# Leftover token blocks of two ranges multiplied as a pair, and a last product moved to the end

## The chip, the cores and the metric

The kernel runs on one core of a Trainium2 chip. Its engines run side by side: TensorE (PE) multiplies matrices, VectorE (DVE) and ScalarE (ACT) read and write tiles, GpSimd (POOL) copies and casts here and issues transfers, SyncE (SP) issues transfers. The metric is the time of one execution on the device in microseconds (us); a kernel's time is the median of several runs.

## The reference

Attention over 8 batches, 12 heads, 448 tokens and head width 64, and behind it a two-layer network on all 3584 tokens (768 to 2048 to 768) with a leaky rectifier:

```python
attn = softmax(q @ k.T / sqrt(64))          # per batch and head
x = (attn @ v) as [3584, 768]               # heads side by side
h = x @ w_in                                # [3584, 2048]
g = np.maximum(0.01 * h, h)
out = g @ w_out                             # [3584, 768]
```

Inputs and output are 32-bit floats; the kernel multiplies in bf16 and adds in 32 bits.

## The kernel before

**Units and clusters.** Attention is cut into 48 units, one pair of heads of one batch each. A unit has four chunks of scores. A *cluster* is a bundle of attention work, put in between the network's matmuls: score matmuls of three chunks (six matmuls of 448 columns into three of the `sc` tiles), their exponentials on ACT (the third one is emitted late, by `settle`), and the products with v of earlier chunks (`pv`, 16 matmuls for each head), which DVE normalises into `x`. Before its scores a unit's q and k are loaded (units below 18 in pairs by POOL's queue, later ones singly by SP's), cast or copied on POOL (`cast`), and transposed: up to unit 13 by PE, from unit 14 by a DMA that SP issues (`turn`). The finished `x` of a unit is transposed into `xT`, from unit 9 on by such a DMA too. SP issues in order; so do its waits.

**Ranges.** The network runs over 8 ranges of tokens, cut at multiples of 128 (`cuts`). Even ranges have 384 tokens (3 blocks of 128), odd ones 512 (4 blocks). For each range, `mlp(i)` first computes h: 16 groups of 6 matmuls (L326) into one of two `g` banks of PSUM, each followed by the rectifier on ACT (L470, in range 0 L458). h is one tile of 4 blocks, allocated anew for each range.

**Second layer.** A block times `w_out` is done in two halves of 384 columns. `blocks` (L438) does it plainly: 16 matmuls of 384 columns for each half, 32 for a block, with a copy by DVE (L442) behind each half. `block_pair` (L367) does two blocks together by Winograd's form of Strassen's scheme: 7 half products of 8 matmuls in place of 8, 56 matmuls in place of 64. For it DVE forms sums and differences of the blocks of h (`mix_h`, L348 to L351, four instructions for four groups of h) and, once, in range 1, of the quarters of the weights (`mix_weights`, L339, 16 instructions into `w_mix`). Seven evictions on DVE (copies L373, additions L376) bring a pair to its two output tiles `o1` and `o2`; there are three `o` buffers, and SP stores them.

Range 0 does its three blocks by `blocks`. The other even ranges (2, 4, 6) do one block by `blocks` and two as a pair; odd ranges are two pairs: 11 pairs and 6 single blocks.

**Order.** The order of PE's work is written out by the program: `mlp` yields after each piece how much it did, and the loop at the end puts the next cluster in when the share of the range's work done reaches the cluster's share. In range 0 it goes by the number of pieces done instead (`early`). A pair can take a cluster after its fourth product (without its value products, which are made up for later) and after its last.

**The end.** In the last pair, the last product goes in two pieces of 192 columns, each with its own copy and its own store, split over ACT's and SP's queues:

```python
            piece(slice(0, NW // 2))
            put(slice(0, NW // 2))
            done = product(a, s4, w_out_sb[:, hi, right])
            join(o1, right, a)
            store(o1, cuts[i] + one.start)
            piece(slice(NW // 2, NW))
            put(slice(NW // 2, NW))
```

Of the kernel before, what the change touches and what calls it, by code (L numbers as in the profile page):

```python
# [10 lines left out]
BF16 = mybir.dt.bfloat16  # L11
AX = mybir.ActivationFunctionType
# [4 lines left out]
def kernel(  # L17
# [9 lines left out]
    nc = tc.nc  # L27

    B, H, S, D = q.shape
    DM, DF = moe_w_in.shape  # L30
    P = 128
# [3 lines left out]
    KD = DM // P  # L35
    MD = DF // P
    NW = DM // 2
# [3 lines left out]
    cuts = [((b * S) // P) * P for b in range(B)] + [B * S]  # L41
# [13 lines left out]
    h_pool = ctx.enter_context(tc.tile_pool(name="h", bufs=1))  # L55
# [30 lines left out]
    w_in_sb = w_pool.tile([P, KD, DF], BF16)  # L86
    w_out_sb = w_pool.tile([P, MD, DM], BF16)
    MH = MD // 2
    w_mix = w_pool.tile([P, 4, MH, NW], BF16)
    h_mix = h_pool.tile([P, 3, MH, 2 * P], BF16, name="hmix")  # L90
    w_in_v = moe_w_in.rearrange("(ko ki) n -> ki ko n", ki=P)
    w_out_v = moe_w_out.rearrange("(ko ki) n -> ki ko n", ki=P)

# [217 lines left out]
    def settle():  # L311
        while late:
            expo(*late.pop(0))
# [17 lines left out]
    def mix_weights():  # L331

        for m in range(0, MH, 2):
            lo, hi = slice(m, m + 2), slice(MH + m, MH + m + 2)
            w11, w12 = w_out_sb[:, lo, :NW], w_out_sb[:, lo, NW:]
            w21, w22 = w_out_sb[:, hi, :NW], w_out_sb[:, hi, NW:]
            t1, t2, t3, t4 = (w_mix[:, x, lo] for x in range(4))
            for o, x, y in ((t1, w12, w11), (t2, w22, t1), (t3, w22, w12), (t4, w21, t2)):
                nc.vector.tensor_sub(o, x, y)  # L339
                yield  # L340

    def mix_h(h, m, nh):

        lo, hi = slice(m, m + 2), slice(MH + m, MH + m + 2)
        h11, h21 = h[:, lo, :nh], h[:, lo, nh:2 * nh]
        h12, h22 = h[:, hi, :nh], h[:, hi, nh:2 * nh]
        s2, s3, s4 = (h_mix[:, x, lo, :nh] for x in range(3))
        nc.vector.tensor_sub(s3, h11, h21)  # L348
        nc.vector.tensor_add(h21, h21, h22)
        nc.vector.tensor_sub(s2, h21, h11)  # L350
        nc.vector.tensor_sub(s4, h12, s2)  # L351

    def block_pair(i, h, c, nh):

        lo, hi = slice(0, MH), slice(MH, MD)
        one, two = ts(c, P), slice(nh + c * P, nh + (c + 1) * P)
        s2, s3, s4 = (h_mix[:, x, :, one] for x in range(3))
        t1, t2, t3, t4 = (w_mix[:, x] for x in range(4))
        left, right = slice(0, NW), slice(NW, DM)
        o1 = o_pool.tile([P, DM], F32, name="o")  # L360
        o2 = o_pool.tile([P, DM], F32, name="o")
        b, a = next_bank(), next_bank()

        def product(ps, x, w, first=False):
            settle()
            for m in range(MH):
                nc.tensor.matmul(  # L367
                    ps[:, :NW], x[:, m], w[:, m], start=(first and m == 0), stop=(m == MH - 1), skip_group_check=True,
                )
            return MH * NW  # L370

        def keep(o, at, ps):
            nc.vector.tensor_copy(o[:, at], ps[:, :NW])  # L373

        def join(o, at, ps):
            nc.vector.tensor_add(o[:, at], o[:, at], ps[:, :NW])  # L376
# [16 lines left out]
        t0 = cuts[i] + two.start  # L393
        if t0 + P == B * S:
            store(o2, t0, right)

            def piece(w):
                settle()
                for m in range(MH):
                    nc.tensor.matmul(  # L400
                        b[:, w], h[:, MH + m, two], t4[:, m, w], start=False, stop=(m == MH - 1),
                        skip_group_check=True,
                    )

            def put(w):
                nc.vector.tensor_copy(o2[:, w], b[:, w])
                store(o2, t0, w, (nc.scalar, nc.sync))

            piece(slice(0, NW // 2))
            put(slice(0, NW // 2))  # L410
            done = product(a, s4, w_out_sb[:, hi, right])
            join(o1, right, a)
            store(o1, cuts[i] + one.start)
            piece(slice(NW // 2, NW))
            put(slice(NW // 2, NW))
            return
        done = product(a, s4, w_out_sb[:, hi, right])
        join(o1, right, a)
        store(o1, cuts[i] + one.start)
# [7 lines left out]
    def blocks(i, h, todo):  # L427

        o = {}
        n = cuts[i + 1] - cuts[i]  # L430
        for c, w in todo:
            settle()
            if c not in o:
                o[c] = o_pool.tile([P, DM], F32, name="o")
            ps = next_bank()
            nw = w.stop - w.start
            for m in range(MD):
                nc.tensor.matmul(  # L438
                    ps[:, :nw], h[:, m, ts(c, P)], w_out_sb[:, m, w],
                    start=(m == 0), stop=(m == MD - 1),  # L440
                )
            nc.vector.tensor_copy(o[c][:, w], ps[:, :nw])  # L442
            t0 = cuts[i] + c * P
            if w.stop == DM:
                store(o.pop(c), t0)
            yield MD * nw, True

    def mlp(i):

        n = cuts[i + 1] - cuts[i]  # L450
        h = h_pool.tile([P, MD, 4 * P], BF16, name="h")
        if i == 0:
            for m in opened:
                part(i, m, (KD - 1,))
            for m in range(MD):
                if m not in opened:
                    part(i, m, range(KD))
                nc.scalar.activation(h[:, m, :n], open_t.pop(m)[:, :n], AX.Prelu, alpha=0.01)  # L458
                settle()
                yield KD * n, True  # L460
            yield from blocks(i, h, [(c, slice(w, w + NW)) for w in (0, NW) for c in range(n // P)])
            return

        nh = n // (2 * P) * P
        weights = mix_weights() if i == 1 else iter(())
        ready = []
        for m in range(MD):
            mm = m // 2 + m % 2 * MH
            part(i, mm, range(KD))
            nc.scalar.activation(h[:, mm, :n], open_t.pop(mm)[:, :n], AX.Prelu, alpha=0.01)  # L470
            settle()
            if ready:
                mix_h(h, ready.pop(), nh)
# [4 lines left out]
        mix_h(h, ready.pop(), nh)  # L478
        for c in range(2 * nh // P, n // P):
            yield from blocks(i, h, [(c, slice(0, NW)), (c, slice(NW, DM))])  # L480
        for c in range(nh // P):
            yield from block_pair(i, h, c, nh)


    def supply(u):
# [106 lines left out]

    begin = [9, 8 * 2 + 3] + [8 * (i + 1) + 5 for i in range(2, B - 1)] + [8 * B + 3]

    early = [4, 6, 8, 10, 12, 14, 16, 18, 20, 22]
    for i in range(B):
        work = list(range(begin[i], begin[i + 1])) if i + 1 < B else []
        n = cuts[i + 1] - cuts[i]
        pairs = n // (2 * P) if i > 0 else 0
        total = MD * KD * n + (n // P - pairs / 4) * MD * DM  # L600
        if i == B - 2:
            total *= 0.75
        used, done, groups = 0, 0, 0
# [50 lines left out]
```

## Time and profile before

| | us |
|---|---|
| median of 3 runs | 408.59 (408.35 to 408.76) |
| the profiled execution | 408.24 |
| its span | 406.5 |
| range 0, from its first group to its end | 31 to 79.8 |
| range 1 | 79.8 to 135.1 |
| range 2 | 135.1 to 178.3 |
| range 3 | 178.3 to 230.0 |
| range 4 | 230.0 to 273.3 |
| range 5 | 273.3 to 325.0 |
| range 6 | 325.0 to 361.7 |
| range 7 | 361.7 to the end |

The span is the time from the first to the last instruction in the profile; the execution's time has some 1.7 us around it. A group of instructions in the profile has a line, an engine, an operation, the tiles it writes and reads, its shape and count, then its busy time, the mean of one in ns, and the idle time in front of it with what ended that. On the chain of waits a row is a start, a length and what ran.

### The profile page before, as it was taken

The numbers are of one execution on the slowest core, as the hardware profiler recorded it, in microseconds if no ns is written. First come the engines' busy times: TensorE is split into PE (matmuls) and PEld (weight loads), VectorE is DVE, ScalarE is ACT, GpSimd is POOL, SyncE is SP. The second block draws the span as 40 slices with busy tenths as digits, with TensorE's granted clock in tenths as the row PEclk, the third lists the DMA queues.
The fourth block names the chain that finished last, engine by engine and source line by source line (L and its number), as shares of the span: only waits on it lengthen the run. The fifth ranks groups of instructions, "written<-read, shape, count | busy, mean of one in ns | idle before, by whom it ended". The sixth has DMA issues, their size and how long they took to land.

```text
span 406.5 us, 9142 instructions
## 1 busy us (share of the span) xinstructions
PE 393.6 (97%) x3655; PEld 228.4 (56%) x3672; DVE 173.0 (43%) x457; ACT 228.3 (56%) x324; POOL 110.0 (27%) x177
## 2 busy tenths in 40 slices
PE   7999999999999999999999999999999999999994
PEld 3566666555555665554555665655455566654562
DVE  3662432465743344334344344443344434323442
ACT  5998872487554776456742677447644476014300
POOL 8786754523312231113112133213110000000000
PEclk9999999999999999999999999999999999999998
DMA  8999999994838784898647678587563411120022
GB/s 129 194 201 205 202 200 127 192 275 110 175 109 207 195 196 97 218 198 139 166 102 170 162 188 159 138 212 178 123 105 101 104 44 24 50 81 0 2 77 77
DMA packets 96586, 57.23 MB, mean 141 GB/s; under 512 B 53280, under 2 KB 93088, under 8 KB 96544
## 3 DMA queue, kind: packets, MB, share of 16 engines
q1 hardware_dynamic: 76848, 44.15, 47.1%
q0 software_dynamic: 19392, 12.26, 21.2%
q8 instruction: 28, 0.46, 0.5%
q10 hardware_dynamic: 304, 0.25, 0.2%
q14 instruction: 14, 0.11, 0.1%
HBM read 45.61 MB, written 11.01 MB: 139 GB/s over the span
## 4 chain that ended last, share of the span: by engine, by line
PE 92%; DVE 3%; ACT 1%; DMA 1%; issue 1%; DVEq 0%; ACTq 0%; POOLq 0%
PE g L326 35%; PE g L367 25%; PE g L271 12%; PE sc L252 10%; PE g L438 8%; PE g L235 1%; ACT e L261 1%; DVE x L279 1%; DMA fq<-in_q_dram 1%; PE g L292 1%; DVE rec L278 1%; PE sc L326 0%; PE g L400 0%; DVE xT L293 0%; DVE qkb L146 0%
## 5 line engine op out<-in xcount | busy, mean ns | idle before, releaser
L261 ACT ACTIVATE e<-sc 112x896 bf16<-112x896 f32 x192 | 165.3, 918 | 88.4 <-PE sc L252 88.1
L326 PE MATMUL g<-xT,w_in_sb 128*128 128x384 bf16 (+1 forms) x739 | 148.8, 352 | 2.2 <-DVE x L279 1.1
L326 PEld LDWEIGHTS <-w_in_sb 128*128 128x128 bf16 x768 | 72.9, 98 | 65.7 <-issue 2.1
L470 ACT ACTIVATE h<-g 128x512 bf16<-128x512 f32 (+1 forms) x112 | 61.9, 552 | 60.0 <-PE g L326 57.6
L271 PEld LDWEIGHTS <-e 112*128 112x128 bf16 x1536 | 56.2, 98 | 22.1 <-issue 15.6
L271 PE MATMUL g<-v,e 112*128 112x65 bf16 x1536 | 64.0, 194 | 0.3 <-ACT e L261 0.2
L252 PE MATMUL sc<-qkT 64*128 64x448 bf16 x384 | 50.0, 353 | 1.1 <-DVE qkT L241 0.6
L146 POOL CAST qkb<-fq 112x512 bf16<-112x512 f32 x30 | 18.6, 621 | 111.0 <-DMA fq<-in_q_dram 82.9
L278 DVE RECIPROCAL rec<-g 112x4 f32<-112x4 f32 x96 | 17.4, 181 | 68.1 <-PE g L271 46.4
L367 PEld LDWEIGHTS <-h 128*128 128x128 bf16 x344 | 33.4, 98 | 22.7 <-issue 0.6
L279 DVE TENSOR_TENSOR x<-g,rec 112x256 bf16<-112x256 f32 x96 | 40.7, 424 | 3.6 <-DVE rec L278 0.3
L373 DVE COPY o<-g 128x384 f32<-128x384 f32 x43 | 24.0, 557 | 29.7 <-PE g L367 29.0
L367 PEld LDWEIGHTS <-hmix 128*128 128x128 bf16 x264 | 25.1, 98 | 19.3 <-issue 3.6
L148 POOL CAST v<-fv 112x512 bf16<-112x512 f32 x30 | 19.1, 636 | 60.8 <-PE g L271 50.6
L438 PE MATMUL g<-w_out_sb,h 128*128 128x384 bf16 x192 | 32.7, 326 | 0.4 <-DVE x L279 0.3
L367 PE MATMUL g<-w_mix,hmix 128*128 128x384 bf16 x176 | 32.3, 326 | 0.0
L367 PE MATMUL g<-w_out_sb,h 128*128 128x384 bf16 x176 | 30.4, 326 | 0.4 <-DVE x L279 0.4
L367 PE MATMUL g<-w_mix,h 128*128 128x384 bf16 x168 | 30.7, 326 | 0.0
L376 DVE TENSOR_TENSOR o<-o,g 128x384 f32<-128x384 f32 x33 | 18.3, 554 | 28.6 <-PE g L367 28.6
L252 PEld LDWEIGHTS <-qkT 64*128 64x128 bf16 x384 | 14.5, 94 | 20.1 <-issue 11.0
L438 PEld LDWEIGHTS <-h 128*128 128x128 bf16 x192 | 18.5, 98 | 12.3 <-issue 0.6
L348 DVE TENSOR_TENSOR hmix<-h 128x512 bf16<-128x512 bf16 (+1 forms) x28 | 11.8, 420 | 31.5 <-ACT h L470 31.5
(50 smaller groups left out, 199.3 us busy)
## 6 DMA issues: line engine op xcount, KB each, us to landing
fk<-in_k_dram SPq DMA_DIRECT2D x31, 224.0 KB, 3.3
fq<-in_q_dram SPq DMA_DIRECT2D x30, 224.0 KB, 3.3
fv<-in_v_dram SPq DMA_DIRECT2D x30, 224.0 KB, 3.8
w_in_sb<-in_moe_w_in_dram POOLq DMA_DIRECT2D x4, 768.0 KB, 11.1
w_out_sb<-in_moe_w_out_dram POOLq DMA_DIRECT2D x4, 768.0 KB, 13.5
out_dram<-o SPq DMA_DIRECT2D x7, 336.0 KB, 3.5
out_dram<-o SPq DMA_DIRECT2D x8, 288.0 KB, 3.9
out_dram<-o SPq DMA_DIRECT2D x8, 240.0 KB, 3.3
```

The source lines that it names most:

```text
L146: by(qk_sb[u][:, x].rearrange("p so h d -> p h so d"), f)
L148: by(v_sb[u % NV][:, :, :, :D], f)
L252: nc.tensor.matmul(ps[:, j, :S], t[j * D:(j + 1) * D, S + c * SC:S + c * SC + P], t[j * D:(j + 1) * D, :S], start=True, stop=True,)
L261: nc.scalar.activation(e[:, :, c, :], sc_t.pop((u, c))[:SC, :, :S], AX.Exp, scale=scale)
L271: nc.tensor.matmul(ps[:, qc, :], e[:, at:at + P], vt[:, j, c, :], start=(c == 0), stop=(c == NSC - 1),)
L278: nc.vector.reciprocal(rec, ps[:SC, :, D:])
L279: nc.vector.tensor_mul(x_t[u][:, :, j, :], ps[:SC, :, :D], rec.to_broadcast([SC, NSC, D]))
L326: nc.tensor.matmul(open_t[m][:, :n], w_in_sb[:, kk, ts(m, P)], xT[:, kk, at:at + n], start=(fresh and kk == kks[0]), stop=(kk == KD - 1),)
L367: nc.tensor.matmul(ps[:, :NW], x[:, m], w[:, m], start=(first and m == 0), stop=(m == MH - 1), skip_group_check=True,)
L373: nc.vector.tensor_copy(o[:, at], ps[:, :NW])
L438: nc.tensor.matmul(ps[:, :nw], h[:, m, ts(c, P)], w_out_sb[:, m, w], start=(m == 0), stop=(m == MD - 1),)
L470: nc.scalar.activation(h[:, mm, :n], open_t.pop(mm)[:, :n], AX.Prelu, alpha=0.01)
```

## The change

The tile h is kept for the whole kernel and has five blocks in place of four, `h[:, :, 0:640]`. Range 0 writes its blocks to slots 2, 3 and 4 and multiplies only the first two. Range 2 writes to slots 0 to 2 and does two pairs: slots (0, 1), and (4, 2), the kept third block of range 0 with its own third. Range 4 writes to slots 2 to 4, does one pair (2, 3), and keeps its third block for range 6, which does as range 2. So there are 13 pairs and 2 single blocks. `spots(i)` gives a range's first slot and its pairs, `token(i, x)` the first token of a slot.

The tile of one weight mixture (t1 = w12 - w11) is no longer separate: DVE writes it over w12 in the right half of `w_out`, after range 0 has used it, and the order of the four mixtures is changed to suit.

The loop's total for a range is counted from its pairs, and the last three entries of `early` are 17, 18, 19 in place of 18, 20, 22.

In the last pair the s4 product comes ahead of both pieces of the last product, and the store of `o1` goes out in two halves.

```diff
-    w_mix = w_pool.tile([P, 4, MH, NW], BF16)
-    h_mix = h_pool.tile([P, 3, MH, 2 * P], BF16, name="hmix")
+    w_mix = w_pool.tile([P, 3, MH, NW], BF16)
+    KEEP = 4
+    h = h_pool.tile([P, MD, (KEEP + 1) * P], BF16, name="h")
+    h_mix = h_pool.tile([P, 3, MH, 2, P], BF16, name="hmix")
...
-            t1, t2, t3, t4 = (w_mix[:, x, lo] for x in range(4))
-            for o, x, y in ((t1, w12, w11), (t2, w22, t1), (t3, w22, w12), (t4, w21, t2)):
+            t2, t3, t4 = (w_mix[:, x, lo] for x in range(3))
+            for o, x, y in ((t3, w22, w12), (w12, w12, w11), (t2, w22, w12), (t4, w21, t2)):
...
-    def mix_h(h, m, nh):
-
+    def spots(i):
+
+        n = cuts[i + 1] - cuts[i]
+        if n == 4 * P:
+            return 0, [(0, 2), (1, 3)]
+        if i == 0:
+            return 2, []
+        return (0, [(0, 1), (KEEP, 2)]) if i % 4 == 2 else (2, [(2, 3)])
+
+    def token(i, x):
+
+        if x == KEEP:
+            return cuts[i - i % 4] + 2 * P
+        return cuts[i] + (x - spots(i)[0]) * P
+
+    def mix_h(i, m):
+
+        at = spots(i)[1]
+        step = [max(1, at[-1][y] - at[0][y]) for y in range(2)]
+        one, two = (slice(at[0][y], at[-1][y] + 1, step[y]) for y in range(2))
         lo, hi = slice(m, m + 2), slice(MH + m, MH + m + 2)
-        h11, h21 = h[:, lo, :nh], h[:, lo, nh:2 * nh]
-        h12, h22 = h[:, hi, :nh], h[:, hi, nh:2 * nh]
-        s2, s3, s4 = (h_mix[:, x, lo, :nh] for x in range(3))
+        t = h.rearrange("p m (c t) -> p m c t", t=P)
+        h11, h21 = t[:, lo, one], t[:, lo, two]
+        h12, h22 = t[:, hi, one], t[:, hi, two]
+        s2, s3, s4 = (h_mix[:, x, lo, :len(at)] for x in range(3))
...
         if t0 + P == B * S:
+            store(o1, token(i, x1), left)
             store(o2, t0, right)
...
-            piece(slice(0, NW // 2))
-            put(slice(0, NW // 2))
-            done = product(a, s4, w_out_sb[:, hi, right])
-            join(o1, right, a)
-            store(o1, cuts[i] + one.start)
-            piece(slice(NW // 2, NW))
-            put(slice(NW // 2, NW))
+            done = product(a, s4, w_out_sb[:, hi, right])
+            join(o1, right, a)
+            store(o1, token(i, x1), right)
+            for w in (slice(0, NW // 2), slice(NW // 2, NW)):
+                for m in range(MH):
+                    nc.tensor.matmul(
+                        b[:, w], h[:, MH + m, two], t4[:, m, w], start=False, stop=(m == MH - 1),
+                        skip_group_check=True,
+                    )
+                nc.vector.tensor_copy(o2[:, w], b[:, w])
+                store(o2, t0, w, (nc.scalar, nc.sync))
...
-            yield from blocks(i, h, [(c, slice(w, w + NW)) for w in (0, NW) for c in range(n // P)])
+            yield from blocks(i, [(first + c, slice(w, w + NW)) for w in (0, NW) for c in range(2)])
...
-        for c in range(2 * nh // P, n // P):
-            yield from blocks(i, h, [(c, slice(0, NW)), (c, slice(NW, DM))])
-        for c in range(nh // P):
-            yield from block_pair(i, h, c, nh)
+        for c in range(len(pairs)):
+            yield from block_pair(i, c)
...
-    early = [4, 6, 8, 10, 12, 14, 16, 18, 20, 22]
+    early = [4, 6, 8, 10, 12, 14, 16, 17, 18, 19]
...
-        pairs = n // (2 * P) if i > 0 else 0
-        total = MD * KD * n + (n // P - pairs / 4) * MD * DM
+        total = MD * KD * n + (len(spots(i)[1]) * 7 / 4 if i > 0 else 2) * MD * DM
```

More of the change, by code (lines that the diff above doesn't have):

```diff
@@ L351, in mix_h, with block_pair @@
         nc.vector.tensor_sub(s4, h12, s2)
-    def block_pair(i, h, c, nh):
+    def block_pair(i, c):
         lo, hi = slice(0, MH), slice(MH, MD)
-        one, two = ts(c, P), slice(nh + c * P, nh + (c + 1) * P)
-        s2, s3, s4 = (h_mix[:, x, :, one] for x in range(3))
-        t1, t2, t3, t4 = (w_mix[:, x] for x in range(4))
+        x1, x2 = spots(i)[1][c]
+        one, two = ts(x1, P), ts(x2, P)
+        s2, s3, s4 = (h_mix[:, x, :, c] for x in range(3))
+        t2, t3, t4 = (w_mix[:, x] for x in range(3))
+        t1 = w_out_sb[:, lo, NW:]
         left, right = slice(0, NW), slice(NW, DM)
@@ L392, in block_pair @@
         yield done, None
-        t0 = cuts[i] + two.start
+        t0 = token(i, x2)
         if t0 + P == B * S:
+            store(o1, token(i, x1), left)
             store(o2, t0, right)
-            def piece(w):
-                settle()
+            done = product(a, s4, w_out_sb[:, hi, right])
+            join(o1, right, a)
+            store(o1, token(i, x1), right)
+            for w in (slice(0, NW // 2), slice(NW // 2, NW)):
                 for m in range(MH):
@@ L403, in piece @@
                     )
-            def put(w):
                 nc.vector.tensor_copy(o2[:, w], b[:, w])
                 store(o2, t0, w, (nc.scalar, nc.sync))
-            piece(slice(0, NW // 2))
-            put(slice(0, NW // 2))
-            done = product(a, s4, w_out_sb[:, hi, right])
-            join(o1, right, a)
-            store(o1, cuts[i] + one.start)
-            piece(slice(NW // 2, NW))
-            put(slice(NW // 2, NW))
             return
@@ L418, in block_pair @@
         join(o1, right, a)
-        store(o1, cuts[i] + one.start)
+        store(o1, token(i, x1))
         yield done, None
@@ L425, in block_pair, with blocks @@
         yield done, True
-    def blocks(i, h, todo):
+    def blocks(i, todo):
         o = {}
-        n = cuts[i + 1] - cuts[i]
         for c, w in todo:
@@ L442, in blocks @@
             nc.vector.tensor_copy(o[c][:, w], ps[:, :nw])
-            t0 = cuts[i] + c * P
+            t0 = token(i, c)
             if w.stop == DM:
@@ L450, in mlp @@
         n = cuts[i + 1] - cuts[i]
-        h = h_pool.tile([P, MD, 4 * P], BF16, name="h")
+        first, pairs = spots(i)
+        hs = h[:, :, first * P:first * P + n]
         if i == 0:
@@ L457, in mlp @@
                     part(i, m, range(KD))
-                nc.scalar.activation(h[:, m, :n], open_t.pop(m)[:, :n], AX.Prelu, alpha=0.01)
+                nc.scalar.activation(hs[:, m], open_t.pop(m)[:, :n], AX.Prelu, alpha=0.01)
                 settle()
                 yield KD * n, True
-            yield from blocks(i, h, [(c, slice(w, w + NW)) for w in (0, NW) for c in range(n // P)])
+            yield from blocks(i, [(first + c, slice(w, w + NW)) for w in (0, NW) for c in range(2)])
             return
-        nh = n // (2 * P) * P
         weights = mix_weights() if i == 1 else iter(())
@@ L469, in mlp @@
             part(i, mm, range(KD))
-            nc.scalar.activation(h[:, mm, :n], open_t.pop(mm)[:, :n], AX.Prelu, alpha=0.01)
+            nc.scalar.activation(hs[:, mm], open_t.pop(mm)[:, :n], AX.Prelu, alpha=0.01)
             settle()
             if ready:
-                mix_h(h, ready.pop(), nh)
+                mix_h(i, ready.pop())
             if m % 4 == 3:
@@ L477, in mlp @@
             yield KD * n, True
-        mix_h(h, ready.pop(), nh)
-        for c in range(2 * nh // P, n // P):
-            yield from blocks(i, h, [(c, slice(0, NW)), (c, slice(NW, DM))])
-        for c in range(nh // P):
-            yield from block_pair(i, h, c, nh)
+        mix_h(i, ready.pop())
+        for c in range(len(pairs)):
+            yield from block_pair(i, c)
     def supply(u):
```

## The prediction

> **What bounds the kernel now.** I read the page first (engines, slices, chain of waits), then the groups by form, the chain in order of time, stage windows, and the timelines of two places.
>
> ```profile
> span 406.5 us, 9142 instructions
> ...
> PE 393.6 (97%) x3655; PEld 228.4 (56%) x3672; DVE 173.0 (43%) x457; ACT 228.3 (56%) x324; POOL 110.0 (27%) x177
> ...
> PEclk9999999999999999999999999999999999999998
> ...
> PE 92%; DVE 3%; ACT 1%; DMA 1%; issue 1%; DVEq 0%; ACTq 0%; POOLq 0%
> ```
>
> PE is busy 97% of the span at the full clock, and 92% of the chain that ends last is PE: a matmul removed is time removed, as long as no other engine makes PE wait at the new places. The groups give each form, the chain gives the pace:
>
> ```profile
> L438 PE MATMUL g<-w_out_sb,h 128*128 128x384 bf16 x192 | 32.7, 326 | 0.4 <-DVE x L279 0.3
> ...
> L373 DVE COPY o<-g 128x384 f32<-128x384 f32 x43 | 24.0, 557 | 29.7 <-PE g L367 29.0 <-DMA fk<-in_k_dram 0.7
> ...
> L376 DVE TENSOR_TENSOR o<-o,g 128x384 f32<-128x384 f32 x33 | 18.3, 554 | 28.6 <-PE g L367 28.6
> ```
>
> ```profile
> 78.28 0.67 PE sc L252 x6
> ...
> 79.84 2.32 PE g L326 x10
> ...
> 252.17 2.60 PE g L438 x16
> ```
>
> One matmul of 384 columns lasts 326 ns, but two overlap: on the chain 16 of them take 2.60 us, 0.1625 us each. That pace is the price, not 326. Six score matmuls take 0.67 us, 0.112 each. The stages that the change shortens, and the tail (columns: window, its length, then the busy time of PE, its weight loads, DVE, ACT and POOL, the clock, DMA share, GB/s):
>
> ```profile
> 59.00:79.80 20.80, 20.76 (x187) 12.63 (x188) 6.32 (x16) 7.05 (x10) 9.50 (x16) 1.00 1.19 169
> ...
> 230.00:273.30 43.30, 42.97 (x425) 26.02 (x426) 18.13 (x52) 27.52 (x41) 11.15 (x19) 1.00 0.74 174
> ...
> 398.10:406.50 8.40, 2.79 (x25) 2.03 (x23) 1.82 (x4) 0.00 (x0) 0.00 (x0) 0.85 0.33 94
> ```
>
> The first is the block part of range 0, the second range 4; in both PE hardly pauses. The third is the tail: 8.4 us with 2.8 of PE.
>
> **Products.** Two single blocks take 64 matmuls, a pair 56. Range 0 loses one of its three blocks (32 matmuls), range 4 its only single block (32); ranges 2 and 6 turn a block and a kept block into a pair (56 in place of 32, so +24). -32+24-32+24 = -16 matmuls, and the compiled instruction lists agree (808 before, 792 after). 16 x 0.1625 = **-2.6 us**. The projection matmuls, scores and value products keep their numbers.
>
> **DVE.** A pair is evicted by 7 instructions, two blocks by 4. Over the ranges: -2, +5, -2, +5, so 6 more at 0.555 = 3.3 us. The mixing in ranges 2 and 6 grows from the 256-element to the 512-element form: by the groups 334+329+366+292 = 1.32 us becomes 484+428+443+425 = 1.78 us per group of four, 8 groups, 3.7 us. Range 2 had 18.1 us of DVE in 43.2 us; 18.1 + 5 x 0.555 + 4 x 0.46 = 22.7 in some 47: hidden under PE. Where it could show is the first pair of range 2 and of range 6, since no single block now lies between the last mixing and the pair. In range 7 the same order stands before: last projection over at 382.41, the sum that the third product needs done at 383.96, third product at 384.94, 0.98 spare. A projection of 384 columns has a shorter activation (492 against 597 ns). I take 0; if the strided slots (0 and 4) doubled the two instructions on that path (2 x 0.43), the spare still covers it. The 16 weight mixings keep number and size. One of four now writes into the projected weights themselves; it waits for range 0's last product, and DVE has already evicted that product, so nothing new waits.
>
> **Range 4.** Eight clusters now share 43.3 - 5.2 = 38.1 us, with 27.5 us of ACT: 72%, so ACT doesn't bound the stage on average. In the new order three clusters stand 18 projection matmuls apart (2.9 us) where there were 24, and two stand together behind the only pair. Three exponentials in a row take 2.53 us on the timeline, three activations 3 x 0.49: 4.0 us of ACT, against 2.9 + 1.9 = 4.8 us from cluster to cluster. Two clusters together stand in range 1 before: 118.26 to 122.74, 4.48 us, against 3.72 for the sum of its pieces (five at 0.51 to 1.25), so 0.76 lost, 0.44 of it a wait for a score bank. Bounds: 0, and 0.44 at each of eight clusters, 3.5. I take **+0.4**, nearest to the double cluster, because three value products now lie between its scores where there were two.
>
> **Range 0, what is late next.** The last three clusters move up by one, two and three half blocks. The third needs the transposed q and k of unit 14, which come by a DMA from SP, behind a cast on POOL, behind a load:
>
> ```profile
> 66.53 0.62 POOL L146 COPY qkb<-fk 112x512 bf16<-112x512 bf16 x1 [2.23 <-DMA fk<-in_k_dram]
> ```
>
> ```profile
> 67.18 1.22 SPq L213 DMA_TRANSPOSE qkT<-qkb  x1
> ```
>
> The load is late (POOL waits for it), so this chain doesn't move up with PE: it was issued at 54.6 and is bound by DMA, whose slices show 9 until 91 us. The transposing DMA is issued at 67.18 and landed 2.9 us later, at 70.08. PE reaches these scores now at 78.28 (first row of the chain above) - 3 x 2.60 = 70.48, and the fifth of the six matmuls, which is the first to read unit 14, at 70.48 + 4 x 0.112 = 70.93. So 8.6 us of cover shrink to **0.85**. Bounds for the landing: 2.3 (shortest DMA transposition I saw, in range 6) to 7.7 us (a pair of them issued at 55.1): a stall of 0, or of 67.18 + 7.7 - 70.93 = 3.95. I take 0: this very transfer took 2.9, and nothing issued before 67.18 changes. Behind it SP now issues unit 11's transposition at 68.4 instead of 73.27, past the first store, which falls behind it; it took 4.4, so 72.8, and range 1 needs it with its sixth matmul at 79.84 - 5.2 + 5 x 0.22 = 75.7: 2.9 us of cover, gone at a landing of 7.3. Three loads of unit 18 follow it, 5 us earlier than before, into the load of unit 16; that unit's scores come in range 1, at 93.03 - 5.2 = 87.8 (the chain again), ten after its load landed (77.1). Transposed PE tiles and the right half of the projected weights have more: the latter was issued by 48.9 and landed in 14.4 us, 63.3, against a first use at 67.4.
>
> **The tail.** Its timeline before:
>
> ```profile
> 398.14 0.55 DVE L376 TENSOR_TENSOR o<-o,g 128x384 f32<-128x384 f32 x1 [0.74 <-PE g L367]
> 398.75 0.82 PE L400 MATMUL g<-w_mix,h 128*128 128x192 bf16 x8 [0.65 <-DVE o L376]
> ...
> 399.41 1.46 PE L367 MATMUL g<-w_out_sb,hmix 128*128 128x384 bf16 x8
> 399.61 0.36 DVE L406 COPY o<-g 128x192 f32<-128x192 f32 x1 [0.91 <-PE g L400]
> ...
> 400.71 0.82 PE L400 MATMUL g<-w_mix,h 128*128 128x192 bf16 x8
> 400.91 0.56 DVE L376 TENSOR_TENSOR o<-o,g 128x384 f32<-128x384 f32 x1 [0.94 <-PE g L367]
> 401.57 0.36 DVE L406 COPY o<-g 128x192 f32<-128x192 f32 x1
> ```
>
> PE idles 0.65 us because the first piece adds into a bank that DVE is still reading. After the change the s4 product stands there (other bank), 398.10 to 399.40, then the first piece to 400.06. But in the compiled list the second piece's first matmul waits for DVE again, and that wait is not there if the copies come behind both pieces: it is for the first copy, of the same bank. So: copy 400.10 to 400.46, second piece 400.52 to 401.34, copy to 401.74, against 401.93: PE and DVE gain 0.2. The rest is DMA: before, the last copy's store stood on SP behind two stores of 768 columns (issued 401.49 and 401.88) and went out at 402.37, landing 2.7 later, at 405.07, 1.4 before the end. Now those two are half as wide and leave at 400.05; the last goes out at 401.78. The first piece's store, of the same 84 KB, landed in 1.9, so between 1.9 and 2.7: landed at 403.7 to 404.5. Gain 0.6 to 1.4 (0.2 if only DVE's part counts); I take **-1.0**.
>
> The Trainium skill (PSUM — Partial Sum Buffer, "PSUM bank collisions raise a hardware error") speaks against cutting the last product in two: accesses of a bank by two engines are to be kept apart by bank, not by address. The 0.65 us row above and the second wait agree. Were pieces of one bank free to overlap, the second would start 0.46 us earlier (400.06 for 400.52) and the sum would be 404.9 in place of 405.4.
>
> **Sum.** -2.6 + 0.4 - 1.0 = -3.2 us. Against the profiled execution (408.24: span 406.5 and 1.7 around it) 405.0; the median of the runs, 408.59, lies 0.35 above it, so the forecast is **405.4**. Its own range, from the bounds: -2.6 - 1.4 = -4.0 against the profiled one is 404.2; -2.6 - 0.2 + 1.5 (0.44 at three or four clusters) = -1.3 against the median is 407.3.
>
> **Rivals.** (a) Range 4 is bound by ACT and banks, at all eight clusters: +3.5 in place of +0.4, 405.4 + 3.1 = 408.5, no change. For it: 27.5 of 38.1 us. Against it: range 1 has 18-matmul stretches and PE waited for ACT only 0.6 us in the whole run. (b) Range 0 starves, and the kernel gets slower: the transposition of unit 14 lands after 7.7 us, like the pair at 55.1, with its k load later by 0.9 (the weight loads landed in 13.5 and 14.4): 3.95 + 0.9 = 4.8 of stall, 405.4 + 4.8 = 410.2. It decides from a landing at 70.93; at 74.1 the gain is gone, 0.8 later the kernel is slower. For it: DMA at 9 tenths there. Against: the 2.9 measured for that transfer. The Trainium skill (TensorE: Matmul & The Clock Gate, Part 1) says the array's clock halves after an idle window of about 3.4 us; a stall of 4.8 would then cost up to some 1.7 more by an estimate from that page (half of such a window), 411.9. The trace shows a lower clock only in the tail (0.85), where PE idles. (c) The tail gives nothing and the DVE work shows at the two first pairs, 0.43 at each: 405.4 + 1.0 + 0.9 = 407.3, faster but by little. That the products don't drop isn't one: the instruction list has them.
>
> **Chances.** Forecast (404.2 to 407.3, with c in it) 0.86, of which c 0.08; a 0.08; b 0.06. Repeated runs lie within 0.4 us; below 0.2%, 0.8 us, I call it no change, so faster is below 407.8, slower above 409.4. Faster: 0.86 and a third of a, 0.89; same: half of a and a little of b, 0.06; slower: 0.05. The range: 403.9 to 407.6, which leaves out most of a and b and something of the sum's own error.
>
> **What would show it.** Right: 16 matmuls of 384 columns fewer; range 0's blocks end near 74.6; no wait of PE for qkT of unit 14 near 70.9; the second tail piece waits for a DVE copy; the last store is issued near 399.6 (402.4 - 2.2 - 0.6). Wrong: PE waiting for DMA between 67 and 77 us, for ACT between 225 and 265, or DVE's mixing late at the first pair of ranges 2 and 6.

## The result, and the profile after

The changed kernel takes 407.19 us (median of 5 runs, 406.46 to 407.59) against 408.59 for the kernel before: 1.4 us less, a ratio of 0.9964 with a 95% interval of 0.9949 to 0.9980. It is faster, by less than half of the 3.2 us of the forecast, and the time lies in the range. The profiled execution took 407.54 us. Its page, engines and chain of waits:

```profile
span 405.8 us, 9155 instructions
...
PE 393.0 (97%) x3656; PEld 227.1 (56%) x3656; DVE 183.6 (45%) x463; ACT 228.3 (56%) x324; POOL 113.4 (28%) x177
...
PE 88%; DVE 6%; ACT 2%; issue 2%; DMA 2%; DVEq 0%; ACTq 0%; POOLq 0%
```

PE's share of the chain fell from 92% to 88% and DVE's doubled from 3% to 6%. That is a hint that PE now waits behind DVE, and not a price: a second profile of the same kernel (e1 below) has 4% for DVE and 7% for DMA. The groups by form, the products and their evictions:

```profile
L390 PE MATMUL g<-w_mix,hmix 128*128 128x384 bf16 x208 | 38.1, 326 | 1.3 <-DVE o L396 1.3
...
L396 DVE COPY o<-g 128x384 f32<-128x384 f32 x51 | 28.4, 557 | 34.4 <-PE g L390 34.4
...
L452 PE MATMUL g<-w_out_sb,h 128*128 128x384 bf16 x64 | 11.1, 326 | 0.3 <-DVE x L281 0.3
```

64 plain matmuls are left of 192. The duration of a product and of a copy (557 ns) is that of before. New is the idle time in the first row: 1.3 us in which a product with a mixed h waits for an eviction. In the kernel before these products waited for nothing:

```profile
L367 PE MATMUL g<-w_mix,hmix 128*128 128x384 bf16 x176 | 32.3, 326 | 0.0
```

To see where the time went I cut both profiled executions at the score matmuls that open the same clusters, and took differences (after less before):

| stage | predicted | measured |
|---|---|---|
| start, up to 16 us (code not touched) | 0 | +0.78 |
| range 0 | -5.2 | -5.19 |
| range 1 | 0 | +0.35 |
| range 2 | +3.9 | +5.45 |
| ranges 3, 5 and 7 | 0 | +0.04 |
| range 4 | -5.2 + 0.4 | -4.90 |
| range 6 | +3.9 | +4.13 |
| tail, from the end of the s3 product | -1.0 | -1.38 |

The rows sum to -0.72, which is the difference of the spans (405.8 - 406.5). The windows of the shortened stages and the tail, with the columns of the windows shown before (length, then PE, its weight loads, DVE, ACT, POOL, clock, DMA share, GB/s):

```profile
59.78:75.40 15.62, 15.58 (x156) 9.50 (x156) 5.28 (x15) 8.46 (x11) 6.20 (x10) 1.00 1.00 141
231.40:269.80 38.40, 37.90 (x394) 22.91 (x394) 16.28 (x49) 26.78 (x41) 10.99 (x19) 1.00 0.80 183
398.83:405.80 6.97, 2.78 (x24) 1.95 (x22) 1.82 (x4) 0.00 (x0) 0.00 (x0) 0.97 0.30 85
```

The block part of range 0 is 5.2 us shorter, and PE fills all but 0.04 us of it. Range 4 went from 43.3 to 38.4 us with 0.5 us of pauses: ACT, at 26.8 of 38.4, doesn't bound it. The tail is shorter by 1.4 us.

The stage that didn't pay is range 2. The chain of waits of the changed kernel at its first pair:

```profile
151.76 0.67 PE sc L254 x6
...
154.91 0.89 DVE hmix L371
...
156.77 2.76 PE g L390 x16
159.53 0.67 PE sc L254 x6
```

From scores to scores it takes 7.77 us. The pieces between, six scores, 16 value products and 32 products, are 0.67 + 0.62 + 5.20 = 6.49. So 1.28 us are lost at one place, and `mix_h`'s third instruction (L371) is on the chain. The timeline there:

```profile
152.89 2.76 PE L390 MATMUL g<-w_out_sb,h 128*128 128x384 bf16 x16
...
153.15 0.18 DVE L280 RECIPROCAL rec<-g 112x4 f32<-112x4 f32 x1 [3.39 <-ACT e L263]
153.37 0.42 DVE L281 TENSOR_TENSOR x<-g,rec 112x256 bf16<-112x256 f32 x1
...
153.71 0.41 DVE L369 TENSOR_TENSOR hmix<-h 128x512 bf16<-128x512 bf16 x1
153.97 0.63 POOL L148 CAST qkb<-fq 112x512 bf16<-112x512 f32 x1 [3.73 <-DMA fq<-in_q_dram]
154.23 0.64 DVE L370 TENSOR_TENSOR h<-h 128x512 bf16<-128x512 bf16 x1
154.90 0.61 POOL L148 CAST qkb<-fk 112x512 bf16<-112x512 f32 x1 [0.30 <-DMA fk<-in_k_dram]
154.91 0.88 DVE L371 TENSOR_TENSOR hmix<-h 128x512 bf16<-128x512 bf16 x1
...
155.82 0.43 DVE L372 TENSOR_TENSOR hmix<-h,hmix 128x512 bf16<-128x512 bf16 x1
156.16 0.55 DVE L396 COPY o<-g 128x384 f32<-128x384 f32 x1
156.77 1.46 PE L390 MATMUL g<-w_mix,hmix 128*128 128x384 bf16 x8 [1.12 <-DVE o L396]
```

Read it in DVE's order. A cluster stands between the last projection and the pair, so DVE first normalises it (L280, L281), then does the last four mixings, and only then evicts the first product (L396), which PE had finished some 1.8 us earlier (two products of 1.3 us each start at 152.89). The third product goes into that product's bank and waits 1.12 us. Two of the mixings take 0.64 and 0.88 us, just where POOL casts at the same time. The other place with the same order in the program is range 6, by when POOL has nothing left to cast:

```profile
343.06 0.42 DVE L281 TENSOR_TENSOR x<-g,rec 112x256 bf16<-112x256 f32 x1
343.40 0.41 DVE L369 TENSOR_TENSOR hmix<-h 128x512 bf16<-128x512 bf16 x1
343.92 0.43 DVE L370 TENSOR_TENSOR h<-h 128x512 bf16<-128x512 bf16 x1
344.38 0.42 DVE L371 TENSOR_TENSOR hmix<-h 128x512 bf16<-128x512 bf16 x1
344.84 0.42 DVE L372 TENSOR_TENSOR hmix<-h,hmix 128x512 bf16<-128x512 bf16 x1
...
345.79 1.46 PE L390 MATMUL g<-w_mix,hmix 128*128 128x384 bf16 x8 [0.22 <-DVE o L396]
```

Here too the normalisation comes first, but all four mixings take 0.41 to 0.43 us and PE waits 0.22. So by this comparison 0.22 of range 2's 1.12 us is the order alone, and most of the rest, 0.22 + 0.46 = 0.68, is two mixings stretched beside POOL.

The tail, timeline of the changed kernel:

```profile
399.96 0.82 PE L425 MATMUL g<-w_mix,h 128*128 128x192 bf16 x8
...
400.82 0.36 DVE L429 COPY o<-g 128x192 f32<-128x192 f32 x1
...
401.24 0.82 PE L425 MATMUL g<-w_mix,h 128*128 128x192 bf16 x8 [0.45 <-DVE o L429]
...
402.09 0.36 DVE L429 COPY o<-g 128x192 f32<-128x192 f32 x1 [0.91 <-PE g L425]
```

The second piece waits 0.45 us for the copy of the first, as the prediction had it from the instruction list. The last copy ends at 402.45, 3.35 us before the end of the span; before, it ended at 401.93, 4.57 before the end. So 1.2 us of the tail's 1.38 are the last store's.

### The profile page after: what moved, and what is told of

Read it like the earlier page. It is cut to its first block, busy times and chain, and to the rows that moved or that the text cites. A ratio compares the mean times of both kernels' runs of the same rounds, so it can differ in the third digit from the quotient of the medians.

```text
span 405.8 us, 9155 instructions
## 1 busy us (share of the span) xinstructions
PE 393.0 (97%) x3656; PEld 227.1 (56%) x3656; DVE 183.6 (45%) x463; ACT 228.3 (56%) x324; POOL 113.4 (28%) x177
## 4 chain that ended last, share of the span: by engine, by line
PE 88%; DVE 6%; ACT 2%; issue 2%; DMA 2%; DVEq 0%; ACTq 0%; POOLq 0%
PE g L328 34%; PE g L390 28%; PE g L273 11%; PE sc L254 9%; PE g L452 3%; ACT e L263 2%; DVE x L281 2%; PE g L237 1%; DMA fq<-in_q_dram 1%; DVE rec L280 1%; PE g L294 1%; DVE hmix L371 1%; DVE o L396 1%; DVE qkb L148 0%; PE sc L328 0%
## 5 line engine op out<-in xcount | busy, mean ns | idle before, releaser
L328 PE MATMUL g<-xT,w_in_sb 128*128 128x512 bf16 (+1 forms) x756 | 149.7, 353 | 1.4 <-DVE x L281 1.1
L390 PE MATMUL g<-w_out_sb,h 128*128 128x384 bf16 x312 | 54.9, 326 | 0.9 <-DVE x L281 0.7
L390 PEld LDWEIGHTS <-h 128*128 128x128 bf16 x408 | 39.7, 98 | 27.3 <-issue 1.3
L280 DVE RECIPROCAL rec<-g 112x4 f32<-112x4 f32 x96 | 17.4, 181 | 78.7 <-PE g L273 34.4
L396 DVE COPY o<-g 128x384 f32<-128x384 f32 x51 | 28.4, 557 | 34.4 <-PE g L390 34.4
L390 PEld LDWEIGHTS <-hmix 128*128 128x128 bf16 x312 | 29.8, 98 | 24.5 <-issue 5.8
L281 DVE TENSOR_TENSOR x<-g,rec 112x256 bf16<-112x256 f32 x96 | 40.8, 424 | 3.3
L390 PE MATMUL g<-w_mix,hmix 128*128 128x384 bf16 x208 | 38.1, 326 | 1.3 <-DVE o L396 1.3
L399 DVE TENSOR_TENSOR o<-o,g 128x384 f32<-128x384 f32 x39 | 21.6, 554 | 32.3 <-PE g L390 32.0
L148 POOL CAST qkb<-fk 112x512 bf16<-112x512 f32 x30 | 20.9, 695 | 3.4 <-DMA fk<-in_k_dram 2.3
L370 DVE TENSOR_TENSOR h<-h 128x512 bf16<-128x512 bf16 (+1 forms) x28 | 12.9, 460 | 15.8 <-ACT h L484 15.4
L390 PE MATMUL g<-w_out_sb,hmix 128*128 128x384 bf16 x104 | 19.0, 326 | 0.0
```

Of the source, the lines that this page charges most:

```text
L148: by(qk_sb[u][:, x].rearrange("p so h d -> p h so d"), f)
L280: nc.vector.reciprocal(rec, ps[:SC, :, D:])
L281: nc.vector.tensor_mul(x_t[u][:, :, j, :], ps[:SC, :, :D], rec.to_broadcast([SC, NSC, D]))
L328: nc.tensor.matmul(open_t[m][:, :n], w_in_sb[:, kk, ts(m, P)], xT[:, kk, at:at + n], start=(fresh and kk == kks[0]), stop=(kk == KD - 1),)
L390: nc.tensor.matmul(ps[:, :NW], x[:, m], w[:, m], start=(first and m == 0), stop=(m == MH - 1), skip_group_check=True,)
```

## The experiments

My theory was that DVE's order at the first pairs ate the gain; the rivals were range 1's copies, the late start, and, for the whole, that the tail brings the gain and the pairs none. Each experiment stands against the kernel before on the same chip.

**e1, the changed kernel again**, no edit: is the late start chance, and do the waits repeat?

> The changed kernel once more, with a second profile. Theory (the lost time sits at fixed places of the new order): against the kernel before, -1.4 us as measured; PE waits some 1.1 us for DVE at the third product of range 2's first pair, and 0.2 us there in range 6. The 0.8 us that the profiled execution lost before 16 us is in code that the change does not touch: if it is chance, this profile has its matmuls for unit 3's transposition at 14.8 us again and not at 15.6. Rival (the new layout of the tiles slows the start): 15.6 again.

406.88 us against 408.47 (12 runs), ratio 0.9963 (0.9946 to 0.9980). The code that had run 0.78 us late comes 0.17 us late in this profile and between 0.41 early and 0.29 late in e2 to e9: that row of the table is chance. Its place can be named: two DVE copies of 112x512 near 14 us took 0.81 and 0.77 us in that execution, 0.28 and 0.52 in the kernel before, which is the 0.78; POOL was issuing loads beside them both times. The waits for the eviction repeat (1.0 and 0.2 us), and so does the 0.35 us in range 1, where DVE and POOL work side by side. Timeline of e1:

```profile
82.57 0.43 DVE L370 TENSOR_TENSOR h<-h 128x512 bf16<-128x512 bf16 x1 [0.87 <-ACT h L484]
82.67 0.80 POOL L148 COPY qkb<-fk 112x512 bf16<-112x512 bf16 x1
83.03 0.71 DVE L371 TENSOR_TENSOR hmix<-h 128x512 bf16<-128x512 bf16 x1
...
85.51 0.42 DVE L281 TENSOR_TENSOR x<-g,rec 112x256 bf16<-112x256 f32 x1
...
85.98 2.75 PE L328 MATMUL g<-xT,w_in_sb 128*128 128x512 bf16 x11 [0.20 <-DVE x L281]
```

POOL's burst of copies lies at 77 to 89 us. It is paced by loads, so it stays while PE now comes there 4.4 to 5.4 us earlier, and DVE's mixings of range 1 fall into it. The normalisation (L281) comes behind them, late, and PE waits.

e1 also shows something that the profile of the changed kernel hid:

```profile
68.14 1.22 SPq L215 DMA_TRANSPOSE qkT<-qkb  x1
...
70.58 0.89 PE L254 MATMUL sc<-qkT 64*128 64x448 bf16 x6
```

Unit 14's transposition is issued at 68.14, and the scores that read it last 0.89 us instead of 0.74. In the profiled execution of the changed kernel its load was early and PE late, so it went out at 65.57 and nothing showed. From these scores to the first ones of range 1 that execution takes 7.00 us; the other kernels with this range 0 take 7.00 to 7.73 (e1 7.37, e2 7.13, e4 7.61, e5 7.31, e6 7.47, e7 7.00, e8 7.73, e9 7.23, e10 7.00, e11 7.00). The cover in range 0 is used up, and costs nothing to 0.7 us from run to run. The scores of unit 14 are only a part of that: they are at most 0.24 us longer (0.98 for 0.74, in e8). The larger part, up to 0.49 us, comes behind them, at the transposition of unit 11's finished `x` that range 1's first projection reads. It took 4.4 us to land in the kernel before and 6.1 to 6.9 in all profiles with the new range 0 but that of e11, where everything was some 5 us later; in e8 it was issued at 69.25 and landed at 75.89, and PE, there since 75.6, waited 0.33 us for it. In e5 unit 14's scores are on time and all of the 0.3 us is this transfer's.

**e2, the pair first.** The group before the pair is yielded so that no cluster may follow it in ranges 2 and 6; the cluster goes into the pair.

```diff
-            yield KD * n, True
+            yield KD * n, None if m == MD - 1 and i in (2, 6) else True
```

> The changed kernel without the cluster (in range 6: the value products) that the new order puts between the last projection and the first pair of ranges 2 and 6; it comes at the next place instead. Theory (DVE normalises that cluster, then mixes, and only then evicts the first product, so the third product waits): the 1.1 us wait in range 2 and the 0.2 us in range 6 vanish, 1.0 to 1.5 us faster than the changed kernel, some 405.9. Rival (the mixing of 512 elements is too slow by itself, whatever stands in front): under 0.4 us faster, PE still waits at the third product. A second rival: the cluster's work collides at its new place, and nothing is gained.

405.34 us (405.02 to 405.52) against 408.47, ratio 0.9918 (0.9905 to 0.9932): 1.5 us faster than e1 on the same chip. Timeline of e2 at the first pair of range 2:

```profile
152.48 0.42 DVE L372 TENSOR_TENSOR hmix<-h,hmix 128x512 bf16<-128x512 bf16 x1
152.83 0.55 DVE L396 COPY o<-g 128x384 f32<-128x384 f32 x1
153.27 0.61 POOL L148 CAST qkb<-fq 112x512 bf16<-112x512 f32 x1 [4.15 <-DMA fq<-in_q_dram]
...
153.44 1.46 PE L390 MATMUL g<-w_mix,hmix 128*128 128x384 bf16 x8
```

DVE starts its mixings without a cluster ahead of them and is through before POOL's cast; the third product doesn't wait. This confirms the place of the loss. For its size the two profiles show somewhat less than the medians: range 2, cut as in the table, takes 47.44 us against 48.08 in e1, and from the last scores of range 6 to the end of the s3 product it is 62.31 against 62.84, together 1.17 us less. Range 2 gains 0.64 where a wait of 1.0 is gone; the cluster costs something at its new place (PE's score matmuls wait 0.9 us for ACT in the run, 0.4 in e1). Another 0.56 us of the difference lies ahead of range 1, in code that the edit leaves as it was. So the cluster's place is worth 1.2 to 1.5 us.

**e3 and e4, the two halves apart.** e3 is the kernel before with the new tail alone; e4 is the changed kernel with the old tail.

> The kernel before with the new tail alone (s4 product ahead of both pieces, o1 stored in halves). Theory: 1.0 to 1.4 us faster than before, 407.3, all of it behind the end of the s3 product (8.35 us to the end before, 7.0 here). Rival (only the 0.2 us of PE and DVE count, the stores land no sooner): 408.4.

> The changed kernel with the old tail. Theory: the pairs bring little by themselves, 16 matmuls (2.6 us) less 1.9 us of new waits, so 0.0 to 0.7 us faster than before: 407.9 to 408.6. Rival (the tail does nothing and the pairs bring it all): as the changed kernel, 407.2.

e3: 407.04 against 408.47, ratio 0.9974 (0.9956 to 0.9992), -1.43 us. e4: 408.31, ratio 0.9999 (0.9983 to 1.0015), -0.16 us, nothing that can be told. Together -1.59, what e1 gained (408.47 - 406.88). As built, the gain is the tail's: the pairs save 2.6 us of products and lose them again, to within the 0.7 us of e4's interval.

**e5, the last mixing behind the first eviction.** If it is only the eviction's place in DVE's order, this mends it as well.

```diff
         keep(o1, left, b)
+        if ready:
+            mix_h(i, ready.pop())
         yield done, None
...
-        mix_h(i, ready.pop())
```

> The changed kernel with the last mixing of each range put behind the eviction of the first product on DVE, in all ranges; the cluster ahead of the pair stays. It asks what the third product of range 2's first pair waits for. Theory (both are late: the eviction, at 156.7, stands behind four mixings, and the third one's sum itself ends at 155.8, 0.3 us after PE could use it): the eviction moves up by some 1.9 us and the sum back by 0.6, so the wait falls from 1.1 to some 0.9 us and no more than 0.3 us is gained in all. Rival (only the eviction's place in DVE's order matters): the wait vanishes, as without the cluster, 405.4.

407.98 against 408.50, ratio 0.9984 (0.9971 to 0.9997): slower than the changed kernel by about 1 us, which neither the theory nor the rival had. Timeline of e5, range 2:

```profile
157.13 0.55 DVE L399 TENSOR_TENSOR o<-o,g 128x384 f32<-128x384 f32 x1
...
157.74 1.46 PE L390 MATMUL g<-w_out_sb,h 128*128 128x384 bf16 x8 [0.42 <-DVE o L399]
```

Now the fourth product waits, for the second eviction, which stands behind the mixings; it does so six times in the run, 2.1 us in all. In range 2 the loss falls from 1.28 to 0.67, but ranges that had lost nothing lose now. So it is not the place of one eviction alone; what fits both kernels is the sum of DVE's work between the last activation and the evictions.

**e6 and e9, the clusters earlier.** The range's total is scaled in ranges 2 and 6, so that one (e6, 0.98) or two (e9, 0.92) projection groups come between the cluster and the pair.

```diff
+        if i in (2, 6):
+            total *= 0.98
```

> The changed kernel with that cluster one projection group earlier in ranges 2 and 6 (the loop's total 2% smaller there), so one group of six matmuls lies between it and the first pair, and no two clusters stand together at the end of range 2. Theory: the waits in ranges 2 and 6 vanish as without the cluster (405.3) and the 0.5 to 0.8 us that two clusters together cost at the end of range 2 don't come back: 404.5 to 405.0. Rival (one group is too little for DVE, which normalises and mixes slower while POOL copies): the third product waits 0.3 to 0.8 us, 405.3 to 406.

> The changed kernel with the clusters of ranges 2 and 6 moved up by one more group, so two projection groups (1.95 us) lie between the last cluster and the first pair. Theory (DVE's normalising, mixing and eviction need that room, also beside POOL's copies): PE waits nowhere at the third product of range 2's first pair, and no clusters stand together at the end of range 2; 0.3 to 0.6 us faster than with one group: 405.0 to 405.3. Rival (the wait there depends on POOL's copies alone, which fall together with the last mixing in any case): 405.6 as with one group.

e6: 405.63 against 408.50, ratio 0.9928 (0.9909 to 0.9947). e9: 405.75 against 408.72, ratio 0.9926 (0.9913 to 0.9940). Both take the gain of e2, and the three can't be told apart; that a second group is worth 0.3 to 0.6 us more isn't seen. e9's profile still has 0.16 us of waiting at the third product of range 2's first pair. e6 loses more there; its timeline:

```profile
153.19 0.61 POOL L148 CAST qkb<-fq 112x512 bf16<-112x512 f32 x1 [3.78 <-DMA fq<-in_q_dram]
153.24 0.84 DVE L370 TENSOR_TENSOR h<-h 128x512 bf16<-128x512 bf16 x1 [0.46 <-ACT h L484]
...
154.20 0.82 POOL L148 CAST qkb<-fk 112x512 bf16<-112x512 f32 x1 [0.39 <-DMA fk<-in_k_dram]
154.58 0.71 DVE L372 TENSOR_TENSOR hmix<-h,hmix 128x512 bf16<-128x512 bf16 x1
...
155.81 1.46 PE L390 MATMUL g<-w_mix,hmix 128*128 128x384 bf16 x8 [0.53 <-DVE o L396]
```

With the normalisation out of the way sooner, two mixings still meet a cast, 0.84 and 0.71 us, and PE waits 0.53. So the cluster's place made up about half of the 1.12 us, and what is left is no more than the two mixings' stretching, 0.42 + 0.29 us.

**e7, a load later** (e6, and unit 18's load issued one cluster later, with unit 19's): does POOL's burst in range 1 come from the order of the loads?

```diff
-            load(u + 5 + r)
+            for n in {17: (), 18: (18, 19)}.get(g, (u + 5 + r,)):
+                load(n)
```

> As the last one, and unit 18's load is issued one cluster later (with unit 19's). Theory (range 1 lost 0.35 us because the three loads of unit 18 now run into unit 16's, whose late landing bunches six units' copies on POOL into 12 us, and DVE's bf16 instructions take 0.7 to 0.95 us beside POOL in place of 0.42 to 0.55): unit 16's k lands earlier than 77.5, POOL's copies spread, the 0.35 us come back, 0.2 to 0.4 us faster than the last one. Rival (DMA is full there whatever the order): no difference.

405.56, ratio 0.9925 (0.9910 to 0.9940), not to be told from e6. Unit 16's k was copied at 74.5 us, 3 us earlier than in e1 and 1.1 earlier than in e6, but POOL still copied back to back from 77.5 to 85.3 us, and the stretch in range 1 stayed at 5.53 us (5.18 before). That theory falls.

**e11, the weights' mixings later** (e9, and range 1's 16 weight mixings begun four groups later): the same 0.35 us from DVE's side.

```diff
-            next(weights, None)
+            for _ in range((m >= 4) + (m in (6, 8, 10, 12))):
+                next(weights, None)
```

> As the one before the last (two groups), with range 1's sixteen weight mixings begun four groups later and then at up to two for a group. Theory (range 1 loses 0.35 us because PE now reaches it 5 us earlier, while the burst of copies on POOL, bound by DMA, stays at 77 to 85 us, and DVE's bf16 instructions take 0.7 to 0.95 us beside it): with fewer of them inside the burst the 0.35 us come back, 0.2 to 0.4 us faster, and the second and third score matmuls of range 1 are 5.2 us apart in place of 5.5. Rival (the delay there is the mixing of h, or something else on PE): no difference, 5.5 us apart.

406.70 against 408.72, ratio 0.9946 (0.9924 to 0.9967): no gain over e9, whose median is 0.95 lower. The stretch that had taken 5.53 us takes 5.17 in its profile, as the theory said; but that execution (411.31 us, 4.6 above the median) was 5 us late by then, so PE came to POOL's burst as late as in the kernel before. Its delay is from the first 25 us: a wait of PE of 2.7 us for a first copy of xT, which stood on DVE behind a copy of 112x512 that took 2.55 us beside three of POOL's (0.29 is usual), and a clock granted at 0.50 (last section). e10, without this edit, has 5.27 there in its profile, where its scores start at 84.5 us against 82.4 to 83.4 in e9, e1 and the changed kernel. e10 was late too, in part by a clock of 0.50 at its start. So this profile can't tell the edit from its lateness. What it does show is a new loss: the two stretches behind take 11.70 together instead of 11.38, with the weight mixings on its chain:

```profile
98.06 0.57 DVE w_mix L341
...
98.65 1.04 DVE w_mix L341 x2
```

So the edit seems to have a cost of its own, 0.32 us, and its gain isn't shown.

**e8 and e10, the tail** (on e6 and e9). e8 does the last product in one piece. e10 cuts the s4 product in half and puts one half ahead of each piece, so that the copy of the first lies beside matmuls of another bank.

```diff
-            for w in (slice(0, NW // 2), slice(NW // 2, NW)):
+            for w in (left,):
```

```diff
-            done = product(a, s4, w_out_sb[:, hi, right])
-            join(o1, right, a)
-            store(o1, token(i, x1), right)
-            for w in (slice(0, NW // 2), slice(NW // 2, NW)):
+            for x in range(2):
+                w = slice(x * NW // 2, (x + 1) * NW // 2)
+                for m in range(x * MH // 2, (x + 1) * MH // 2):
+                    nc.tensor.matmul(
+                        a[:, :NW], s4[:, m], w_out_sb[:, MH + m, right], start=False, stop=(m == MH - 1),
+                        skip_group_check=True,
+                    )
+                if x:
+                    join(o1, right, a)
+                    store(o1, token(i, x1), right, (nc.scalar, nc.sync))
```

> As the one before the last (cluster one group earlier), with the last product in one piece of 384 columns behind all others. Theory: the two pieces in one bank can't overlap, since the second waits 0.45 us for the copy of the first; in one piece PE and DVE end some 0.35 us earlier, but the last store carries 168 KB in place of 84 and lands 0.3 us later by the rows of the tail (2.2 against 1.9): no difference within 0.2 us. Rival (two pieces hide the first half's store): 0.5 us slower.

> As the last one, with the s4 product cut into two halves of four matmuls, one ahead of each piece of the last product, and half of o1's store on ACT's queue. Theory: the first half covers the addition, the second half the first copy, so the 0.45 us wait of the second piece vanishes and the last copy ends 0.55 us earlier; the last store too: 0.3 to 0.6 us faster than the last one. Rival (the last store's issue stands behind o1's on SP and gains nothing): within 0.1 us.

e8: 405.43, ratio 0.9924 (0.9903 to 0.9945), the same as e6: cutting the product in two gains nothing that shows. e10: 405.70, ratio 0.9935 (0.9912 to 0.9957), the same as e9. In its timeline the second piece no longer waits:

```profile
399.92 0.81 PE L423 MATMUL g<-w_out_sb,hmix 128*128 128x384 bf16 x4
400.12 0.36 DVE L435 COPY o<-g 128x192 f32<-128x192 f32 x1 [0.91 <-PE g L431]
...
400.57 0.82 PE L431 MATMUL g<-w_mix,h 128*128 128x192 bf16 x8
```

The 0.45 us are gone from PE, and the last copy ends 3.18 us behind the s3 product instead of 3.63. From the end of that product to the end of the span it is 6.63 us against 6.94 in e9 (and 6.68 in e8 against 6.94 in e6), one profile each, but the medians don't show it. Whether it is worth anything is open.

The fastest kernel of these is e2, though e6, e8 and e9 lie within its uncertainty; all beat both the kernel before and the changed one.

## Why the prediction was right in sign and wrong in size

**The step that failed** is in the paragraph on DVE: "since no single block now lies between the last mixing and the pair. In range 7 the same order stands before ... 0.98 spare ... I take 0". The place was right, the price wrong: 1.12 us of waiting at the first pair of range 2 and 0.22 at that of range 6; by stages, 1.55 and 0.23 us over the +3.9 of each. It is one of the signs that the prediction itself names for being wrong.

First, the spare was read from the wrong row. The third product needs not only its sum, done at 383.96, but also the bank of the first product, which DVE empties behind the last mixing. Range 7 of the kernel before:

```profile
384.34 0.55 DVE L373 COPY o<-g 128x384 f32<-128x384 f32 x1
...
384.94 1.46 PE L367 MATMUL g<-w_mix,hmix 128*128 128x384 bf16 x8
```

That copy ends at 384.89: the spare was 0.05 us and not 0.98, so what DVE does more, or more slowly, in that stretch, PE waits for. Second, range 2 differs from range 7 in two ways. In range 7 attention is over, so no cluster stands between the last projection and the pair and DVE has none to normalise; in range 2 one does, as the list of PE's instructions showed. And in range 7 POOL is idle, so the mixings took 0.42 us there; in range 2 two of them took 0.64 and 0.88. I also counted DVE's work over the whole stage ("22.7 in some 47: hidden under PE"). An average says nothing of the 3 us in which it decides. e2 gives most of the loss back (1.2 to 1.5 us) by taking away the cluster alone; e5 shows that moving one eviction doesn't.

**Products**, -2.6 us: right. 792 matmuls are left (312 + 208 + 104 + 96 at L390, 64 at L452, 16 of half width at L425), and range 0 fell by 5.19 for a predicted 5.2.

**Range 4**, +0.4 for denser clusters: measured 0.30. Rival (a), all eight clusters bound by ACT, did not occur.

**Range 0**, "I take 0": right in the profiled execution, too good by some tenths in others. Unit 14's transposition landed in 2.9 us again (e1, e8), but where it is issued at about 68.1 the scores are up to 0.24 us longer: the mechanism of rival (b), at its very edge. The other term, "it took 4.4, so 72.8 ... 2.9 us of cover", was mis-sized: unit 11's transposition was issued near 69 and took 6.1 to 6.9, so that the cover was gone in some executions, which cost up to 0.49 us. Together 0 to 0.7 us and not 4.8. No such stall occurred in range 0, but what the clock does behind a wait can be seen at the start of e10 and e11 (last section), and not as the rule cited in rival (b) has it.

**Range 1**: I checked the transfers that would be late there, and not what DVE and POOL would do side by side once PE comes 5 us earlier. 0.35 us, not foreseen. That POOL's copies cause it is argued from e1's rows, and from e10 and e11, which came there later and lost 0.09 us and nothing; no edit brought it back.

**Tail**, -1.0: measured -1.38 in the trace and -1.43 in e3. PE's and DVE's part came as worked out: the last copy ends 3.62 us behind the s3 product, predicted 3.64. The last store landed nearer to the good bound. The Trainium skill's rule (PSUM — Partial Sum Buffer, "PSUM bank collisions raise a hardware error"), to keep two engines apart by bank, agrees with the 0.45 us wait, and with e10, where the wait goes as another bank's matmuls stand between. The wait is one that the compiled program asks for; no run here lets two engines into one bank.

**Rival (c)** had the place of the loss, at 0.43 us for each first pair; it had the tail wrong. Its time, 407.3, is close to the measured 407.19 by luck: it has too little loss at the pairs, none in range 1 and no gain in the tail, and these errors nearly cancel.

The sum: -3.2 forecast, +1.78 at the first pairs, +0.35 in range 1, -0.38 and -0.10 in tail and range 4 make -1.55; e1 measured -1.59.

## What to carry to other kernels

When an edit takes work out from between two steps of the bounding engine, list what the helping engines must do, in their own order, in the few microseconds between those steps; a stage's average, or a place that looks the same with the neighbours idle, doesn't price it. Split a change of two parts and measure each: here the small one brought everything, and one line in the order of the other brought most of its worth back. Where a spare is read off a trace, take it from the last thing that the waiting instruction needs, the free buffer as well as the operand. A stream that is paced by loads stays where it is when the engine that bounds the kernel gets faster, so look at what the shift now lays side by side.

## What the hardware showed that I had not expected

DVE and POOL slow each other, depending on what DVE reads. Over the profiles of all 13 runs, a bf16 DVE operation of 128x512 from SBUF to SBUF took 0.41 to 0.43 us in each of the 919 cases with POOL copying nothing at the time (range 6 above). Of 201 that ran beside POOL's copies for more than half of their time, 125 took over 0.5 us, up to 0.88; the others took 0.41 to 0.5, as the one at 82.57 in e1 (0.43). POOL's copies and casts of 112x512 took at most 0.65 us where DVE ran no bf16 operation; of 232 that had one from SBUF to SBUF beside them for more than half of their time, 141 took over 0.7 us, up to 1.68. Operations that read PSUM kept their time: 1248 normalisations took at most 0.43 us and 1211 evictions of 128x384 at most 0.56, 581 and 106 of them beside POOL's copies for more than half of their time. The Trainium skill (GPSIMD Engine Reference, "2. Architecture") says that GpSimd's ports to SBUF are shared with DVE; the rows agree, and the page gives no price for it. That the port is the cause is argued from these rows and was not tested by itself.

PE's clock can halve behind waits of about a microsecond. In e10 the granted clock was 0.50 from 13.7 to 17.1 us, in e11 from 10.7 to 14.2 and from 17.6 to 24.4 us, and four score matmuls took 0.93 us there in place of 0.55. In the 3.4 us ahead of these falls PE had been busy for 2.05, 1.97 and 1.67 us, with waits of 0.86, 1.01 and 2.69 us (the last one went on beyond the fall). A wait of 0.83 us near 15 us in the changed kernel's first profile left the clock at 1.00. So the idle window of about 3.4 us, in the rule that the prediction cites from the Trainium skill, wasn't needed in these runs.

Still open: what would remove range 1's 0.35 us, whether e10's shorter tail is real, and which of e2, e6 and e9 is best.
